# A decode kernel's K and V in pieces of 48, 32 and 48 KB over a ring lapped twice per head

## Chip, cores and metric

One core of one Trainium2 chip. The metric is the device time of one launch in microseconds (us), the median of the runs. Each run also gives the span, from the first to the last instruction that the profile counts.

## The reference, cut to what matters

One token of a transformer block: layer norm, grouped-query attention over a cache of 65,536 positions, an output projection and a small gated feed-forward part. Eight K/V heads serve 32 query heads.

```python
Hq, Hkv, Sk, Dh = 32, 8, 65536, 128
q = (layernorm(x) @ wq)                       # one token
scores = einsum("bhqd,bhkd->bhqk", q, k) * Dh ** -0.5
o = einsum("bhqk,bhkd->bhqd", softmax(scores), v)
h = x + o @ wo
h2 = h + (sigmoid(n @ w_gate) * (n @ w_up)) @ w_down      # n = layernorm(h)
```

K and V of a head are 16 MB each; with eight heads and the weights 282 MB have to be read, each byte once.

## The kernel before

The SP engine issues all loads, in one fixed order, on one queue. K and V come in blocks of 4 MB (32 KB per partition) into a ring of four slots; K of one head is interleaved with V of the head before.

```python
order = [("wq", 0)]
order += [("K", b) for b in range(NR)]                    # NR = 4 blocks per head
for b in range(NR, NB):
    order += [("K", b), ("V", b - NR)]
order += [("V", NB - 4), ("V", NB - 3), ("V", NB - 2), ("V", NB - 1), ("wg", 0), ("wu", 0), ("wd", 0)]
# ... slot i % 4; a load waits for the user of the load four places earlier:
def freed(ld):
    k, b = ld
    return {"wq": "q", "K": f"F{b}", "V": f"PV{b}"}[k]    # K: transposed by DVE; V: multiplied by PE
```

VectorE (DVE) transposes K chunk by chunk (a chunk is 4 KB per partition; 8 to a block), TensorE (PE) multiplies them with q into scores; after four blocks the maxima are taken and the exponentials made; in the next head's time PE multiplies the transposed probabilities with V, two chunks to a round, four rounds to a block:

```python
# PE, for each head i and block r of four:
#   scores of K block (i, r)                    32 matmuls of 128x512
#   if r == 3: maxima, exponentials (section X)
#   PV of V block (i - 1, r)                    4 rounds of 8 matmuls
# ... DVE, for each chunk c of a block b:
op("dve", lambda e: e.transpose(dst, src), deps, f"T{b}.{c}", to="T")
# ... after the last one:
op("dve", lambda e: e.memset(scr[:, b:b + 1], 0.0), (), f"F{b}")   # the mark that frees the slot
```

At the end, the last four V blocks take slots of V blocks two places earlier; wo goes into the space of the transposed K; then the gate, up and down weights.

Of the kernel before, what the change touches and what calls it, by code (L numbers as in the profile page):

```python
# [13 lines left out]
HKV = 8  # L14
GS = 4
NQ = 32
DH = 128
# [18 lines left out]
class Prog:  # L36
# [26 lines left out]
    def emit(self):  # L63
# [3 lines left out]
        needed = {d for ops in self.ops.values() for o in ops for d in o["deps"]} | set(self.at_end)  # L67
# [20 lines left out]
        for e, ops in self.ops.items():  # L88
            n = 0
            for o in ops:  # L90
                if o["dma"]:
                    k, v = o["dma"]
                    value[o["name"]] = (self.dma_sems[k]["sem"], v, k)
                elif o["to"]:
                    k = o["to"]
                    counts[k] = counts.get(k, 0) + 1
                    if o["name"]:
                        value[o["name"]] = (extra[k], counts[k], k)
                    o["inc"] = True
                elif o["name"] in needed or o.get("inc"):  # L100
                    n += o["times"]
                    value[o["name"] or id(o)] = (sems[e], n, e)
                    o["inc"] = True
# [110 lines left out]
def bass_sequential_preLN__gqa_block_cached__glu_gated_glu__decode_kernel(  # L214
# [10 lines left out]
    SLOT = T * DH  # L225
    CH = TC * DH
    NF = FF // 128
# [6 lines left out]
    with ExitStack() as es:  # L234
# [16 lines left out]
        ring = sb("ring", [128, NSLOT * SLOT], bf16)  # L251
# [50 lines left out]
        def slot_ap(s):  # L302
            return ring[:, s * SLOT:(s + 1) * SLOT]

# [4 lines left out]
        order = [("wq", 0)]  # L309
        order += [("K", b) for b in range(NR)]  # L310
        for b in range(NR, NB):
            order += [("K", b), ("V", b - NR)]
        order += [("V", NB - 4), ("V", NB - 3), ("V", NB - 2), ("V", NB - 1), ("wg", 0), ("wu", 0), ("wd", 0)]
        slot_of, prev = {}, {}
        for i, ld in enumerate(order):
            if ld[0] == "V" and ld[1] >= NB - NR:
                slot_of[ld] = slot_of["V", ld[1] - 2]
                prev[ld] = ("V", ld[1] - 2)
            elif ld[0][0] == "w" and i:
                slot_of[ld] = 3 if ld[0] == "wd" else 1  # L320
                prev[ld] = ("K", NB - 1 if ld[0] == "wd" else NB - 2)
            else:
                slot_of[ld] = i % NSLOT
                prev[ld] = order[i - NSLOT] if i >= NSLOT else None

        def freed(ld):
            if ld is None:
                return None
            k, b = ld
            return {"wq": "q", "K": f"F{b}", "V": f"PV{b}"}[k]  # L330

        dma("act", lambda e: e.dma_start(x_col[:, :], A_x[0].rearrange("o (p k) -> (o p) k", k=4)), "x", name="x")
        V_SPLIT = [(0, 3), (3, 4)]
        W_SPLIT = {"wg": [(0, 4)], "wu": [(0, 3), (3, 4)]}
        W_AT = {"wg": 0, "wu": 4 * FF}
        for ld in order:
            k, b = ld
            s = slot_of[ld]
            dst = slot_ap(s)
            deps = [freed(prev[ld])]  # L340
            if k == "wq":
                dma("sp", lambda e, d=dst: e.dma_start(d.rearrange("p (k n) -> p k n", k=4),
                    A_wq.rearrange("(p k) n -> p k n", p=128)), f"r{s}", deps, "wq")
            elif k in ("wg", "wu"):
                w = B_w_gate if k == "wg" else B_w_up
                dst, src = dst[:, W_AT[k]:W_AT[k] + 4 * FF], w.rearrange("(p k) n -> p (k n)", p=128)
                for i, (k0, k1) in enumerate(W_SPLIT[k]):
                    dma("sp", lambda e, d=dst, w=src, a=k0 * FF, z=k1 * FF: e.dma_start(d[:, a:z], w[:, a:z]),
                        f"{k}{i}", deps if i == 0 else (), f"{k}.{i}")
            elif k == "wd":  # L350
                src = B_w_down.rearrange("(p r) n -> p r n", p=128)
                for i, (r0, r1) in enumerate(WD_SPLIT):
                    dma("sp", lambda e, d2=dst[:, r0 * D:r1 * D].rearrange("p (r n) -> p r n", n=D), sr=src[:, r0:r1, :]:
                        e.dma_start(d2, sr), f"wd{i}", deps if i == 0 else (), f"wd{i}")
            else:
                h, r = b // NR, b % NR
                cache = A_k_cache if k == "K" else A_v_cache
                src = cache[0, h, r * BLK:(r + 1) * BLK, :].rearrange("(p t) d -> p (t d)", t=T)
                if ld == ("V", NB - 1):
                    for i, (c0, c1) in enumerate(V_SPLIT):  # L360
                        d2, s2 = (ap[:, 2 * c0 * CH:2 * c1 * CH] for ap in (dst, src))
                        dma("sp", lambda e, d2=d2, s2=s2: e.dma_start(d2, s2),
                            "v0" if i else "vl", deps if i == 0 else (), f"V{b}.{i}")
                else:
                    dma("sp", lambda e, d=dst, sr=src: e.dma_start(d, sr), f"v{s}" if k == "V" else f"k{s}" if k == "K" and b >= NR else f"r{s}",
                        deps, f"{k}{b}")
            if ld == ("V", NB - 4):
                for i, (j0, nj) in enumerate(WO):
                    src = A_wo[j0 * DH:(j0 + nj) * DH, :].rearrange("(p r) n -> p (r n)", r=nj)
                    dst = ktw[:, j0 * D:(j0 + nj) * D]  # L370
                    dma("sp", lambda e, src=src, dst=dst: e.dma_start(dst, src), f"wo{i}",
                        [f"G{HKV - 1}"] if i == 0 else (), f"wo{i}")
# [81 lines left out]
        def project_q(e):  # L454

            e.reg_mov(reg(e, 0), addr_of(xz, 8 + 7))
            e.reg_mov(reg(e, 4), addr_of(ring, slot_of[("wq", 0)] * SLOT))
# [3 lines left out]
            with e.Fori(0, HKV):  # L461
                for kt in range(4):
                    mm_at(e, ps(1, 0, 512, 0, 8), at_reg(xz, reg(e, kt), [[4 * 16, 128], [1, 8]]),
                          at_reg(ring, reg(e, 4 + kt), [[NSLOT * SLOT, 128], [1, 512]]), False, 32)
# [36 lines left out]
        def dve_block(b):  # L501
            s = slot_of[("K", b)]
            for c in range(NC):
                n = b * NC + c
                at = s * SLOT + (2 * (c % NR) + c // NR) * CH
                src = ring[:, at:at + CH].bitcast(fp32)
                dst = ktw[:, (n % NKT) * CH:(n % NKT + 1) * CH].bitcast(fp32)
                deps = [f"K{b}"] if c == 0 else []
                if b % NR or b == 0:
                    deps.append(f"S{b - 1}.{c}" if b else None)  # L510
                op("dve", lambda e, d=dst, sr=src: e.transpose(d, sr), deps, f"T{b}.{c}", to="T")  # L511
            op("dve", lambda e: e.memset(scr[:, b:b + 1], 0.0), (), f"F{b}")
# [62 lines left out]
        def pv_regs(e):  # L575
            for half in range(NC // NR):
                for tq in range(4):
                    i = 8 * half + tq
                    if i:
                        e.reg_alu(reg(e, i), R["p"], 2 * (128 * tq + half), ALU.add)  # L580
                        e.reg_alu(reg(e, i + 4), R["v"], 2 * (half * TC + 4 * tq) * 128, ALU.add)

        def pv(b):
            h, r = b // NR, b % NR
            if r == NR - 1:
                P.part["pe"] = ("VL", b)
                op("pe", lambda e: None, [f"V{b}" if b < NB - 1 else f"V{b}.1"])
            P.part["pe"] = ("B", b)
            for half in range(NC // NR):
                for tq in range(4):  # L590
                    i = half * 8 + tq
# [3 lines left out]
                        at_reg(ring, reg(e, i + 4) if i else R["v"], [[NSLOT * SLOT, 128], [1, 512]]), False, 32, 32 * tq),  # L595
                       (), f"PV{b}" if half and tq == 3 else None, times=NR)

        def head_out(h):
            op("act", lambda e: e.activation(po_sb[:, :], ps(PO, 0, 512), AF.Copy, scale=rl[:, :]),  # L599
               [f"PV{NR * h + NR - 1}", f"rl{h}"], f"po{h}", to="po")  # L600
# [68 lines left out]
        def pe_flow(e, section):  # L669
# [7 lines left out]
            i, w, p, v, m, k = (R.setdefault(n, e.alloc_register(f"r_{n}")) for n in "iwpvmk")  # L677
            w0, p0 = addr_of(ktw, W0 + NC - 1 + 127), addr_of(PT_sb, 31 * 4)
            v_even, v_odd = (addr_of(ring, slot_of[("V", b)] * SLOT) for b in (0, 1))
            e.reg_mov(i, 0)  # L680
            goto("head")
            e.reg_mov(w, w0)
            e.reg_mov(p, p0)
            goto("part")
# [13 lines left out]
            e.reg_mov(m, NR)  # L698
            e.reg_mov(k, 0)
            e.reg_mov(v, v_even)  # L700

            def odd_late():
                e.reg_mov(v, v_odd)
                e.reg_mov(m, NR - 1)
                e.reg_mov(k, 1)
                away("br_eq", i, HKV, "last_values", lambda: section("VZ"), "sums")
                section("V3")

            def odd():
                e.reg_mov(v, v_odd)  # L710
                section("V1")

            away("br_eq", w, w0, "values0", lambda: section("V0"), "sums")
            away("br_eq", w, w0 - 4, "values1", odd, "sums")
            away("br_eq", w, w0 - 12, "values3", odd_late, "sums")
# [5 lines left out]
            e.reg_alu(p, p, 2 * 512, ALU.add)  # L721
# [5 lines left out]
            def rest():  # L727
                pv_regs(e)
                e.reg_mov(m, 1)
# [7 lines left out]
            e.reg_alu(p, p, 4 - 2 * NR * 512, ALU.add)  # L737
# [7 lines left out]
            away("br_eq", w, w0 - 4, "rows_of_o", lambda: section("L"))  # L745
# [126 lines left out]
```

## Time and profile before

| | before |
|---|---|
| time, median of the runs | 658.86 us (658.33 to 659.61) |
| span of the profiled run | 657.1 us |
| data read | 282.33 MB |
| share of 16 DMA engines' span on the data queue | 99.7% |
| PE, DVE busy | 64%, 53% |
| idle DMA time between the first and the last load (packet records), sum per engine | under 0.5 us |

The last row is from the trace's record of each DMA packet (start, duration, size). One packet here is one partition's row of a transfer; 128 packets, eight to each of 16 engines, make a transfer. The record does not name the engine; a packet that starts where another ended is taken to be on the same one. I call *lead* the time from the issue of a transfer to its first packet, and *spread* the time between its first packets on the first and on the last of the 16 engines. With a full queue the lead is long because a transfer stands behind others. The lines of the profile that carry the reading are in the prediction below.

### The profile page before, as it was taken

The page shows a single profiled execution, that of the slowest core. Times are in us where ns is not written, and L with a number is a line of the kernel's source. Part 1 is how long each engine was busy: PE and PEld are TensorE (multiplying, and loading weights), DVE is VectorE, ACT ScalarE, POOL GpSimd, SP SyncE. Part 2 cuts the span into 40 slices and gives each one's busy share as a digit, 9 for nine tenths or more (in the row PEclk, how much of TensorE's full clock was granted, in tenths as well). Part 3 has the DMA queues.
Part 4 walks back from the last instruction along what each step waited for, and adds up shares of the span by engine and source line. Part 5 has one row for each costly group of instructions (what it writes and reads, how often), then busy time and mean ns, then how long its engine had stood idle before and what let it go on. Part 6 is the DMA issues. An engine that isn't in the chain of part 4 may idle for free. (4 is left out here: it accounts for less than half of the span.)

```text
span 657.1 us, 6111 instructions
## 1 busy us (share of the span) xinstructions
PE 420.5 (64%) x2315; PEld 74.1 (11%) x1547; DVE 349.7 (53%) x439; ACT 42.9 (7%) x114; POOL 3.6 (1%) x17
## 2 busy tenths in 40 slices
PE   0688488548666585576765575764866668556746
PEld 0200011011000010010100110101100001001322
DVE  2399775547537665347555374465743575542202
ACT  1100200020000200020000200002000100002001
POOL 1000000000000000000000000000000000000000
PEclk9989689677888697776966769765888869677676
DMA  9999999999999999999999999999999999999998
GB/s 383 447 433 429 439 423 431 431 447 415 447 415 447 437 425 447 415 447 419 443 441 421 447 415 447 423 439 443 419 447 415 447 427 435 445 417 427 435 430 352
DMA packets 10802, 282.34 MB, mean 430 GB/s; under 512 B 1329, under 2 KB 1330, under 8 KB 1842
## 3 DMA queue, kind: packets, MB, share of 16 engines
q1 hardware_dynamic: 10658, 282.33, 99.7%
q10 hardware_dynamic: 144, 0.00, 0.0%
HBM read 282.33 MB, written 0.00 MB: 430 GB/s over the span
## 5 line engine op out<-in xcount | busy, mean ns | idle before, releaser
L431 PE MATMUL PS<-ktw 128*128 128x512 bf16 x1024 | 299.9, 442 | 157.4 <-DVE ktw L511 153.6
L511 DVE STREAM_TRANSPOSE ktw<-ring 128x1024 f32<-128x1024 f32 x256 | 291.6, 1205 | 128.0 <-DMA ring<-in_A_k_cache_dram 128.0
L431 PE MATMUL PS<-ring,PT_sb 128*32 x1024 | 83.9, 455 | 23.6 <-issue 13.2
L431 PEld LDWEIGHTS PS<-ktw 128*128 x256 | 27.1, 106 | 408.2 <-issue 256.8
L565 DVE STREAM_TRANSPOSE PT_sb<-P_sb 128x512 bf16<-128x512 bf16 x32 | 20.2, 684 | 54.0 <-PE PS L602 52.3
L551 ACT ACTIVATE negmax<-PS 128x1 f32<-128x1 f32 x8 | 1.4, 171 | 520.6 <-PE PS L549 520.6
L431 PEld LDWEIGHTS PS<-ring,PT_sb 128*32 x1024 | 25.8, 116 | 79.8 <-issue 74.6
L516 DVE TENSOR_REDUCE M_sb<-PS 128x1 f32<-128x512 f32 x32 | 19.9, 684 | 25.5 <-PE PS L431 25.5
L555 ACT ACTIVATE P_sb<-PS,negmax 128x512 bf16<-128x512 f32 x32 | 21.6, 686 | 0.3
L572 DVE TENSOR_REDUCE lsum<-PS 128x1 f32<-128x4 f32 x8 | 1.3, 163 | 31.2 <-PE PS L570 31.2
L542 PE MATMUL PS<-identf,gm 128*1 128x128 f32 x16 | 3.4, 301 | 16.9 <-DVE gm L540 16.9
L616 DVE TENSOR_TENSOR Lw<-O,blk_of 128x896 bf16<-128x896 bf16 (+1 forms) x2 | 1.4, 683 | 20.6 <-ACT O L606 20.6
L402 PE MATMUL PS<-st,onesf 128*128 128x2 f32 x4 | 1.2, 362 | 16.1 <-DVE st L401 16.1
L431 PE MATMUL PS<-ring,xz 128*8 x32 | 9.2, 459 | 2.3 <-issue 2.3
L599 ACT ACTIVATE po_sb<-PS,rl 128x512 bf16<-128x512 f32 x8 | 5.5, 687 | 53.2 <-PE PS L431 53.2
L431 PE MATMUL PS<-ktw,O 128*1 x26 | 7.6, 464 | 0.0
L549 PE MATMUL PS<-one_f,gmrep 1*128 1x1 f32 x16 | 4.2, 330 | 5.0 <-DVE gmrep L546 5.0
L555 ACT ACTIVATION_READ_ACCUMULATOR P_sb<-PS,negmax 128x1 f32 x32 | 6.5, 202 | 0.0
L476 DVE STREAM_TRANSPOSE qt<-qh 32x512 bf16<-32x512 bf16 x1 | 0.7, 699 | 10.6 <-ACT qh L473 10.6
L602 PE MATMUL PS<-sel_bf,po_sb 128*128 128x4 bf16 x32 | 2.0, 168 | 6.4 <-ACT po_sb L599 6.4
L417 DVE CAST hT<-x_col 128x4 f32<-128x4 bf16 x1 | 0.2, 171 | 10.6 <-DMA x_col<-in_A_x_dram 10.6
L661 DVE COPY yr<-PS 1x512 f32<-1x512 f32 x1 | 0.7, 679 | 8.3 <-PE PS L659 8.3
(82 smaller groups left out, 74.0 us busy)
## 6 DMA issues: line engine op xcount, KB each, us to landing
ring<-in_A_k_cache_dram SPq DMA_DIRECT2D x32, 4096.0 KB, 28.7
ring<-in_A_v_cache_dram SPq DMA_DIRECT2D x31, 4096.0 KB, 26.4
ring<-in_A_wq_dram SPq DMA_DIRECT2D x1, 4096.0 KB, 12.3
ktw<-in_A_wo_dram SPq DMA_DIRECT2D x1, 3584.0 KB, 12.7
ring<-in_A_v_cache_dram SPq DMA_DIRECT2D x1, 3072.0 KB, 13.2
ring<-in_B_w_gate_dram SPq DMA_DIRECT2D x1, 1792.0 KB, 19.0
ring<-in_B_w_up_dram SPq DMA_DIRECT2D x1, 1344.0 KB, 21.7
ring<-in_A_v_cache_dram SPq DMA_DIRECT2D x1, 1024.0 KB, 15.2
```

What stands on the lines that cost most here:

```text
L431: return e.add_instruction(mybir.InstMatmult(name=nc.get_next_instruction_name(), engine=mybir.EngineType.PE, ins=[rhs, lhsT], outs=[e.low ...
L511: op("dve", lambda e, d=dst, sr=src: e.transpose(d, sr), deps, f"T{b}.{c}", to="T")
L516: op("dve", lambda e, u=u: e.tensor_reduce(M_sb[:, u % 4:u % 4 + 1], ps(u % NS, 0, 512), AX.X, ALU.max), [f"S{b}.{NC - NR + k}"], f"mx{u}" ...
L542: op("pe", lambda e: e.matmul(ps(MISC, 0, 128, 0, 1), lhsT=gm[:, :], rhs=identf[:, :], start=True, stop=True), [f"gm{h}"], f"gmT{h}", to="Q")
L549: op("pe", lambda e: e.matmul(ps(MISC, 128, 129), lhsT=gmrep[0:1, :], rhs=one_f[0:1, 0:1], start=True, stop=True), [f"gmrep{h}"], f"neg{h}")
L551: op("act", lambda e: e.activation(negmax[:, k:k + 1], ps(MISC, 128, 129), AF.Copy, scale=-att_scale), [f"neg{h}"], f"negmax{h}")
L555: op("act", lambda e, b=b: e.activation(P_sb[:, (b % 4) * 512:(b % 4 + 1) * 512], ps(b % NS, 0, 512), AF.Exp, bias=negmax[:, k:k + 1], sca ...
L565: op("dve", lambda e, b=b: e.transpose(PT_sb[:, (b % 4) * 512:(b % 4 + 1) * 512], P_sb[:, (b % 4) * 512:(b % 4 + 1) * 512]), [f"E{b}", f"o ...
L572: op("dve", lambda e: e.tensor_reduce(lsum[:, :], ps(MISC, 132, 136), AX.X, ALU.add), [f"l{h}"], f"ls{h}", to="D")
L599: op("act", lambda e: e.activation(po_sb[:, :], ps(PO, 0, 512), AF.Copy, scale=rl[:, :]), [f"PV{NR * h + NR - 1}", f"rl{h}"], f"po{h}", to ...
L602: op("pe", lambda e, t=t: e.matmul(ps(OX, 0, 4), lhsT=po_sb[:, t * 128:(t + 1) * 128], rhs=sel_bf[:, 8 * t:8 * t + 8:2], start=(t == 0), s ...
L616: op("dve", lambda e: e.tensor_tensor(Lw[i][:, :].rearrange("p (j c) -> p j c", j=n), bass.AP(tensor=O2, offset=j0, ap=[[NQ, 128], [1, n], ...
```

## The change

Intent: fewer, larger transfers (six per head instead of eight), in pieces that fill a 128 KB ring exactly when it is lapped twice per head. In each lap a slot is taken again as soon as its readers are through: the first piece of V waits only until two of six rounds of the last PV group have read the end of its slot.

```diff
-        order = [("wq", 0)]
-        order += [("K", b) for b in range(NR)]
...
+    PIECES = ((0, 12), (12, 20), (20, 32))                       # chunks: 48, 32, 48 KB
+    RING = 32 * CH
+    AT = {"K": (0, 24, 8), "V": (12, 0, 20), "K0": (0, 12, 20), "wq": 24, "wg": 12, "wd": 8}
...
+        for h in range(1, HKV + 1):
+            old = h - 2
+            before_k = (["F0.1"], ["G0"], [f"F{h}.1"]) if h == 1 else ([f"PV{old}.2"], [f"PV{old}.3"], [f"F{h}.1"])
+            before_v = (["F0.3"] if h == 1 else [f"PV{old}.3:2"], [f"F{h}.0"], [f"F{h}.2"])
+            if h < HKV:
+                for q in range(3):
+                    load("K", h, q, before_k[q], ("ka", "kb", "ka")[q], f"K{h}.{q}")
+                    load("V", h - 1, q, before_v[q], ("va", "vb", "va")[q], f"V{h - 1}.{q}")
+                continue
+            load("V", h - 1, 0, before_v[0], "va", f"V{h - 1}.0")
...          (wo)
+            load("V", h - 1, 1, (), "vb", f"V{h - 1}.1")
+            for i, cols in enumerate(LAST):
+                load("V", h - 1, 2, [f"PV{h - 1}.1"] if i == 0 else (), f"v{i}", f"V{h - 1}.2{'ab'[i]}", cols)
...
-            op("dve", lambda e: e.memset(scr[:, b:b + 1], 0.0), (), f"F{b}")
+                mark = {7: 0, 11: 1, 19: 2}.get(j, 3 if b == 2 and c == 7 else None)      # j: chunk in the head
+                if mark is not None:
+                    op("dve", lambda e, m=4 * h + mark: e.memset(scr[:, m:m + 1], 0.0),
+                       [f"S{b}.{c}"] if h and mark in (1, 2) else (), f"F{h}.{mark}")
...
+        PARTS = (4, 2, 4, 6)          # PV rounds after the scores of blocks 0 to 3 (were 4 each)
...
             section("B")
-            e.reg_alu(p, p, 2 * 512, ALU.add)
+            e.reg_alu(p, p, s, ALU.add)
+            e.reg_alu(s, s, step[0] ^ step[1], ALU.bitwise_xor)
```

`PV3.3:2` reads: after the second round of the fourth PV group of head 3. Scores are still made in blocks of eight chunks, so K.2 (chunks 20 to 31) brings the second half of block 2 and all of block 3.

## The prediction

> **What bounds the kernel now.** I read the page's DMA rows first, because 282 MB in 657 us is close to what 16 engines can move at all.
>
> ```profile
> span 657.1 us, 6111 instructions
> PE 420.5 (64%) x2315; PEld 74.1 (11%) x1547; DVE 349.7 (53%) x439; ACT 42.9 (7%) x114; POOL 3.6 (1%) x17
> ...
> DMA  9999999999999999999999999999999999999998
> GB/s 383 447 433 429 439 423 431 431 447 415 447 415 447 437 425 447 415 447 419 443 441 421 447 415 447 423 439 443 419 447 415 447 427 435 445 417 427 435 430 352
> ...
> q1 hardware_dynamic: 10658, 282.33, 99.7%
> ```
>
> No compute engine is above 64%; the DMA row is full in every slice and the one queue that carries the data fills 99.7% of 16 engines' span. The swing between 415 and 447 GB/s is no slack: packets of 32 KB are booked whole into 16 us slices. I also added up the trace's packet records: between the first packet at 1.0 us and the last weight packet at 654.6 us there is no time with an idle DMA engine. So nothing can be won except bytes (unchanged) or cost per packet; a lot can be lost if the queue ever runs dry. Next, who sets when a transfer is issued (the DMA queue's own waits):
>
> ```profile
> SPq L365 <- DVE scr L512: 324.2, 30, 19.4
> SPq L365 <- PE PS L431: 222.4, 29, 18.8
> ```
>
> The issuer waits 547 us in all for slots: for DVE (K transposed) and for PE (V multiplied). These waits are harmless as long as other transfers are queued. The issues' times to landing say how many are: 28.7 us for a K block, 26.4 for a V block, where one 4 MB transfer takes 9.7. That is nearly two others ahead. Pairing the issues with the packet records, the shortest leads (issue to first packet) are 4.2 us for the tenth transfer and 3.6 us for wo; most are 12 to 23. Then the timeline near the end, where the change will matter:
>
> ```profile
> 560.10 19.44 SPq L365 DMA_DIRECT2D ring<-in_A_v_cache_dram  x2
> 564.43 9.13 DVE L511 STREAM_TRANSPOSE ktw<-ring 128x1024 f32<-128x1024 f32 x8 [9.48 <-DMA ring<-in_A_k_cache_dram]
> ...
> 566.85 0.59 PE L431 MATMUL PS<-ktw 128*128 128x512 bf16 x1 [0.51 <-DVE ktw L511]
> 567.98 0.59 PE L431 MATMUL PS<-ktw 128*128 128x512 bf16 x1 [0.54 <-DVE ktw L511]
> 569.11 7.97 PE L431 MATMUL PS<-ktw 128*128 128x512 bf16 x29 [0.54 <-DVE ktw L511]
> ...
> 577.00 2.17 PE L431 MATMUL PS<-ring,PT_sb 128*32 x32
> ...
> 583.83 9.13 DVE L511 STREAM_TRANSPOSE ktw<-ring 128x1024 f32<-128x1024 f32 x8 [10.27 <-DMA ring<-in_A_k_cache_dram]
> ...
> 596.39 2.48 DVE L516 TENSOR_REDUCE M_sb<-PS 128x1 f32<-128x512 f32 x4 [3.42 <-PE PS L431]
> ...
> 602.45 2.76 PE L431 MATMUL PS<-ring,PT_sb 128*32 x24 [1.75 <-issue]
> ...
> 606.57 8.66 SPq L365 DMA_DIRECT2D ring<-in_A_v_cache_dram  x2
> ```
>
> Two transposes that each start on a K landing are 19.40 us apart, with one K and one V transfer between: 9.70 us per 32 KB per partition, 0.303 us per KB. A chunk (4 KB) is transposed in 9.13/8 = 1.14 us. The second issue of the first line, at 579.2 us (the row's end), is the first V block of head 7: it takes the slot that the products at 577.00 have freed, well before the last V block of head 6 has landed (593.2). Lastly the chain of waits at the end: after the last V piece it is some 13 us of small PE, ACT and DVE steps beside the landing of the weights, which ends at 654.6, so both meet.
>
> **What the Trainium skill says.** "DMA: Bandwidth & Descriptors", section "Where 436 GB/s comes from", puts the fabric ceiling at 435.2 GB/s for 16 ports; the page's mean of 430 agrees. Same page, "Anatomy of one DMA": a semaphore wait happens on the issuing sequencer and "the SDMA engines just consume their queues"; so a blocked issue blocks all issues behind it, as SPq's waits here do. Same page, "Why small descriptors are slow": a fixed overhead per packet. The records agree: 24,576 B take 912 ns and 32,768 B 1213 ns, so 27.2 bytes per ns and 9 ns fixed. "TensorE: Matmul & The Clock Gate", Part 1: the array falls to half clock when idle and needs sustained work to leave it. Here the windows show a granted 0.50 for 8 to 9 us after each late K landing, then 1.00.
>
> **The change part by part.**
> Removed: 16 of the 64 K and V transfers (six per head for eight). A transfer of 8 packets per engine takes 9.685 us at the steady pace, its bytes at 27.2 per ns 9.632, so 53 ns are fixed: 16 x 0.053 = 0.85 us saved, on the bounding engines, if a 48 KB row stays one packet. If it is cut in two, that becomes a loss of about 0.5.
> Moved off the path: PV rounds are regrouped 4, 2, 4, 6 (16 as before); a register operation more per round; transposes wait in two marks for PE. None of this fills the DMA.
> Added, and decisive: which work must be done before a transfer may be issued. In the ring a head's order is K.0, V.0, K.1, V.1, K.2, V.2 (48, 48, 32, 32, 48, 48 KB; V of the head before). K.0 waits for the third group of products, V.0 for two rounds of the last group, both behind the processing of K.2. From T, the start of K.2's transposes, I rebuild it with durations of before:
> 1. 16 score matmuls of K.2's first four chunks: four start with their transposes (the last at T+4.7, from 564.43 to 569.11), then 12 more with the clock rising. The 29-matmul group lasts 7.6 to 9.1 us over the heads against 6.3 at full clock (0.217 each), so 5 to 13 run at 0.427: done at T+8.5 to 10.2, mean T+9.4.
> 2. Four PV rounds, 2.2: T+11.6. Here K.0 of the next head may go.
> 3. PE's turn from PV back to scores, 0.8 (it is so after each PV block, 104.05 to 104.83 for one): T+12.4. Then 32 matmuls at 0.217 = 7.0: T+19.4. The 12 transposes end at T+13.7, so they don't bound.
> 4. The maxima start 0.6 before the last score: T+18.8. From the first maximum to the first PV matmul of the last group 596.39 to 602.45 = 6.06: T+24.9.
> 5. Two rounds, 16 of 24 matmuls that took 2.76 = 1.84: T+26.7. Issue to first packet about 1.0 (the first load): T+27.7. T is 0.34 after the last byte of K.2, so 28.1 after it.
> In the middle of the run two 48 KB pieces (V.2, next K.0) lie between K.2's end and V.0: 2 x 14.5, less 0.3 by which transfers overlap, = 28.7. It fits with 0.6 us to spare; K.0's wait (11.6 + 1.0 + 0.3 = 12.9 against 14.2) with 1.3. Only late clock rises (0.8 over the mean) give gaps of 0.2 us: 0.3 us in all.
> In the last round there is no next K.0. V.0 of head 7 follows V.2 of head 6 at once, and still waits for those two rounds: 28.1 needed, 14.2 there. The DMA engines stand idle for 13.9 us. wo and V.1 stand behind it in the same queue. Restart: the first transfer of the run took 10.6 from its first packet to the next one's, not 9.7: 0.9. Afterwards the stream is without gaps (V.2's wait for PV.1 ends some 6 us after V.0 lands, with wo and V.1, 19 us, still to move), so all is shifted to the end; the final chain changes by perhaps 0.1.
> Sum: 13.9 + 0.9 + 0.3 - 0.85 - 0.1 = 14.1; 659.4 + 14.1 = 673.5 us.
>
> **The rivals.**
> First, hidden anyway: the pieces keep the engines fed everywhere and the time falls by the 0.85 us of packets, to 658.5. For it: every lead of before is above 3.5 us, and the ring has the same 128 KB. Against: V.0's slot in the last round holds the end of K.2 and the start of V.2, which can't be free earlier than 12 transposes (13.7 us) after K.2 lands, and that alone exceeds the budget.
> Second, a wait in each head: if path 1 to 5 is 1 us longer than I have it, six heads lose some 0.4 us each besides the last, which loses 1.0: 677. For it: spare of 0.6 us, and PE's clock is the least certain term. Against: the steps are taken from spans that recur within 0.2 us in all heads except the clock's rise.
> Third, PE becomes the bound, since groups of six rounds and half-block scores make it wait in larger lumps. Against: 64% busy, and at half clock for much of it; its backlog is gone by the next K.2, where it waits some 9 us. That would need over 77 us of work per head, and there are some 52. I give it little.
> Fourth, a 48 KB row pitch makes reading faster or slower. The packet times of 24, 28 and 32 KB rows lie on one line; I expect 1.81 us for 48 KB.
>
> **Range and chances.** 2% slower begins at 672.6, 0.9 us below the estimate. The clock (plus or minus 0.7), the restart (0.5) and the fixed steps (0.6) give about 1.1; errors upward are amplified by the second rival. So 671 to 677 in 8 of 10. Chances: faster 0.01 (nothing to win there), within 2% 0.31, slower 0.68.
>
> **What would show it.** In the profile after: one slice near 600 us with DMA far under 9, the others full; idle time of 13 to 15 us between V.2 of head 6 and V.0 of head 7; SPq's V.0 issue about 27 us after the start of K.2's transposes in each head; all other leads at least 1 us; 48 KB packets of 1.81 us. It would be wrong if the dip were missing, or came in each head, or if PE's clock did not rise within the first half-block.

## The result

The changed kernel takes 698.31 us (697.58 to 699.18, 4 runs), before 658.86 us. The ratio is 1.0598 (95% interval 1.0578 to 1.0619); a ratio is the mean time of one kernel's runs over that of the other's in the same rounds, so it is not quite the quotient of the medians. It is slower, as I thought likelier, but by 39.5 us where I had worked out 14.1, and outside my range.

The rows of the page of the changed kernel that answer to those of before:

```profile
span 697.7 us, 6265 instructions
...
DMA  9999999899999999999999999999999999918997
GB/s 421 417 446 414 436 375 428 364 409 431 444 417 409 404 426 445 375 397 425 442 426 380 417 424 443 423 380 403 441 434 392 395 431 439 434 82 333 421 429 335
...
q1 hardware_dynamic: 8354, 282.33, 95.5%
```

The same bytes in fewer packets (8,354 for 10,658), and a queue at 95.5%. One slice has nearly no traffic: that is the predicted dip at the end. But ten of the other slices have 364 to 404 GB/s, where before had none under 415 between its first and last slice. The loss looks small in the share (4%) because the slow packets, of which more below, count as busy.

The waits of the DMA queue:

```profile
SPq L324 <- DVE scr L500: 304.2, 23, 15.2
SPq L324 <- PE PS L416: 293.7, 20, 35.9
```

The waits for PE grew from 222 to 294 us, and one of them is 35.9 us long. It is V.0 of head 7, as the timeline at the end shows (start, duration, engine, instruction):

```profile
594.62 36.56 SPq L324 DMA_DIRECT2D ring<-in_A_v_cache_dram  x2
602.87 13.76 DVE L497 STREAM_TRANSPOSE ktw<-ring 128x1024 f32<-128x1024 f32 x12 [8.28 <-DMA ring<-in_A_k_cache_dram]
...
612.69 1.60 PE L416 MATMUL PS<-ring,PT_sb 128*32 x24
...
622.75 2.48 DVE L505 TENSOR_REDUCE M_sb<-PS 128x1 f32<-128x512 f32 x4 [6.12 <-PE PS L416]
...
628.79 4.61 PE L416 MATMUL PS<-ring,PT_sb 128*32 x40 [1.73 <-PEq L171]
631.23 0.91 SPq L343 DMA_DIRECT2D ktw<-in_A_wo_dram  x2
```

The two issues of the first line are V.2 of head 6 at 594.6 and V.0 of head 7 at 630.9, two PV rounds after 628.79. What that does to the DMA engines is plain in a table by stretch, whose last two columns are the share of the 16 engines and GB/s:

```profile
594.00:608.00 14.00, 2.71 (x8) 0.21 (x2) 5.19 (x6) 0.00 (x0) 0.00 (x0) 0.66 1.01 435
608.00:618.00 10.00, 8.66 (x53) 1.30 (x37) 8.62 (x8) 0.00 (x0) 0.00 (x0) 0.79 0.58 251
618.00:632.00 14.00, 9.53 (x57) 1.70 (x41) 3.14 (x8) 2.95 (x9) 0.00 (x0) 0.78 0.13 39
632.00:646.00 14.00, 2.87 (x30) 0.98 (x22) 3.81 (x7) 1.35 (x3) 0.00 (x0) 0.62 0.94 400
```

The chain of waits now runs through it as well, where before it was all small steps of the compute engines:

```profile
628.79 2.05 PE PS L416 x12
630.84 0.02 issue
630.86 17.74 DMA ring<-in_A_v_cache_dram
```

That explains some 14 us, as predicted. The other 25 are in the heads. Here is head 2 in the changed kernel, from K.2's landing; it is the quickest of the seven:

```profile
198.87 13.63 DVE L497 STREAM_TRANSPOSE ktw<-ring 128x1024 f32<-128x1024 f32 x12 [9.91 <-DMA ring<-in_A_k_cache_dram]
...
203.55 4.14 PE L416 MATMUL PS<-ktw 128*128 128x512 bf16 x13 [0.54 <-DVE ktw L497]
207.62 1.60 PE L416 MATMUL PS<-ring,PT_sb 128*32 x24
209.61 0.63 PE L416 MATMUL PS<-ring,PT_sb 128*32 x8 [0.39 <-issue]
210.28 0.33 SPq L324 DMA_DIRECT2D ring<-in_A_k_cache_dram  x1
211.24 7.10 PE L416 MATMUL PS<-ktw 128*128 128x512 bf16 x32 [1.00 <-DVE ktw L497]
217.73 2.48 DVE L505 TENSOR_REDUCE M_sb<-PS 128x1 f32<-128x512 f32 x4 [5.22 <-PE PS L416]
...
223.77 6.00 PE L416 MATMUL PS<-ring,PT_sb 128*32 x48 [1.93 <-PEq L171]
225.83 0.33 SPq L324 DMA_DIRECT2D ring<-in_A_v_cache_dram  x1
```

Counted from T = 198.87, the start of the transposes, the next K.0 is issued at T+11.4 and V.0 at T+27.0. I had worked out T+11.6 and T+26.7, so in this head the path of compute was right to 0.3 us. The other heads are later. In head 4, for example, the two issues come at T+12.6 and T+28.1:

```profile
360.24 13.76 DVE L497 STREAM_TRANSPOSE ktw<-ring 128x1024 f32<-128x1024 f32 x12 [8.23 <-DMA ring<-in_A_k_cache_dram]
...
372.87 0.33 SPq L324 DMA_DIRECT2D ring<-in_A_k_cache_dram  x1
...
388.37 0.33 SPq L324 DMA_DIRECT2D ring<-in_A_v_cache_dram  x1
```

Over heads 1 to 6 the means are T+12.2 and T+27.8, so V.0 is 1.1 us later than I had it. That alone can't account for the loss in a head, as e6 and e7 will show. Each head takes more: V.0 of heads 1 and 6 are issued at 146.7 and 549.1 us, 80.5 us per head, against 77.5 (256 KB at 0.303).

The packet records show what happens at these two issues. All 16 engines were busy with V.2 when K.0 was issued at 210.28; the fastest of them got its first packet of K.0 at 211.28, just when it had finished. The first packets of that transfer took mostly 2.1 to 2.8 us each, where 1.815 is normal, and the 16 engines started on it over 1.7 us. The table pools the transfers of 24 KB rows and more (without each run's first one) of all 14 traces, by lead:

| lead | transfers | packet time over normal, us per engine and transfer | spread (median), us |
|---|---|---|---|
| under 1.3 us | 74 | 0.77 | 1.5 |
| 1.3 to 2.5 | 18 | 0.42 | 2.1 |
| 2.5 to 4 | 49 | 0.02 | 1.05 |
| over 4 | 640 | 0.006 | 1.05 |

In the kernel before the spread is 0.3 us, no transfer after the first has a lead under 2.5, and no packet is slow. In the changed kernel 14 transfers have a lead under 1.3 (K.2 of head 1, K.0 of heads 2 to 7, and every V.0 from head 1 on) and their spread is 0.7 to 3.3 us. Through the last head it stays at 3.2 to 3.5 us.

### The profile page after: what moved, and what is told of

It is laid out like the page before. It is cut to its first block, busy times and chain, and to the rows that moved or that the text cites. A ratio compares the mean times of both kernels' runs of the same rounds, so it can differ in the third digit from the quotient of the medians.

```text
span 697.7 us, 6265 instructions
## 1 busy us (share of the span) xinstructions
PE 425.4 (61%) x2315; PEld 69.9 (10%) x1547; DVE 350.4 (50%) x432; ACT 42.9 (6%) x114; POOL 3.6 (1%) x17
## 3 DMA queue, kind: packets, MB, share of 16 engines
q1 hardware_dynamic: 8354, 282.33, 95.5%
## 5 line engine op out<-in xcount | busy, mean ns | idle before, releaser
L416 PE MATMUL PS<-ktw 128*128 128x512 bf16 x1024 | 295.3, 438 | 171.8 <-DVE ktw L497 166.8
L416 PE MATMUL PS<-ring,PT_sb 128*32 x1024 | 91.0, 462 | 44.1 <-PEq L171 25.3
L416 PEld LDWEIGHTS PS<-ring,PT_sb 128*32 x1024 | 21.7, 116 | 118.4 <-issue 114.9
L500 DVE MEMSET scr<- 1x1 f32 x25 | 1.5, 59 | 45.6 <-PE PS L416 45.6
L587 ACT ACTIVATE po_sb<-PS,rl 128x512 bf16<-128x512 f32 x8 | 5.5, 687 | 77.5 <-PE PS L416 77.5
L461 DVE STREAM_TRANSPOSE qt<-qh 32x512 bf16<-32x512 bf16 x1 | 0.7, 699 | 11.3 <-ACT qh L458 11.3
## 6 DMA issues: line engine op xcount, KB each, us to landing
ring<-in_A_wq_dram SPq DMA_DIRECT2D x1, 4096.0 KB, 12.2
ring<-in_B_w_gate_dram SPq DMA_DIRECT2D x1, 1792.0 KB, 28.1
```

Source lines behind the costliest of these rows:

```text
L416: return e.add_instruction(mybir.InstMatmult(name=nc.get_next_instruction_name(), engine=mybir.EngineType.PE, ins=[rhs, lhsT], outs=[e.low ...
L500: op("dve", lambda e, m=4 * h + mark: e.memset(scr[:, m:m + 1], 0.0), [f"S{b}.{c}"] if h and mark in (1, 2) else (), f"F{h}.{mark}")
L587: op("act", lambda e: e.activation(po_sb[:, :], ps(PO, 0, 512), AF.Copy, scale=rl[:, :]), [f"PV{h}.{NR - 1}", f"rl{h}"], f"po{h}", to="po")
```

## The experiments

**Theory.** Two things cost: the idle stretch at the end, some 14 us, and in each head two issues that come when the queue is all but empty. Such an issue costs some 1.5 us even where it comes in time for its first packet (estimated from the loss: 25 us over 14 to 16 such issues). **Rival A**: rows of 48 KB are slow in themselves. **Rival B**: the regrouped PV rounds, with one register operation more each, bound PE and so the heads. In the table, lost time is the sum over the profiled run, per engine, of idle time between the first and last load and of packet time over normal; leads count transfers of 24 KB rows and more. The times of before were 658.3 to 658.9 us in all rounds.

| run | time, us | ratio to before | mean span, us | leads under 1.3 us | idle + slow, us |
|---|---|---|---|---|---|
| before | 658.9 | 1 | 657.0 | 0 | 0.4 + 1.2 |
| after | 698.3 | 1.060 | 697.0 | 14 | 28.6 + 13.5 |
| e1_tail | 687.1 | 1.045 | 683.0 | 11 | 10.2 + 13.2 |
| e2_early | 678.6 | 1.029 | 676.5 | 3 | 18.0 + 3.9 |
| e3_both | 667.6 | 1.016 | 663.5 | 2 | 3.2 + 2.5 |
| e4_six | 712.3 | 1.082 | 711.0 | 12 | 44.0 + 11.3 |
| e5_ahead | 662.2 | 1.006 | 658.2 | 0 | 0.4 + 1.1 |
| e6_four | 670.3 | 1.017 | 665.0 | 6 | 4.3 + 5.6 |
| e7_sixclean | 675.4 | 1.027 | 670.9 | 6 | 8.7 + 6.1 |
| e8_v0free | 674.3 | 1.023 | 672.5 | 7 | 7.6 + 7.9 |
| e9_late6 | 666.3 | 1.012 | 664.8 | 6 | 3.3 + 4.8 |
| e10_late5 | 664.2 | 1.009 | 662.5 | 4 | 2.2 + 3.1 |
| e11_late4 | 659.4 | 1.003 | 658.5 | 0 | 0.4 + 0.9 |
| e12_halves | 669.0 | 1.016 | 664.4 | 3 | 4.7 + 4.5 |

(The mean span of before is of its runs beside the first four experiments, 656.8 to 657.4.) One thing in the table no view explains: in e1, e3, e5, e6, e7 and e12 the time is mostly 4.4 to 5.4 us above the span, in the others mostly 1.3 to 2.4. These six have the moved V of the last head, with a few more register operations on PE. The difference lies outside what the profile counts, so for them I go by spans. Some of these kernels also scatter more from run to run: the spans of e3 lie between 661.0 and 666.9, those of e6 between 661.8 and 667.1, where before stays within 656.7 and 657.4. The packet records are of one run of each.

**e1_tail.** The last head's V goes where the next K would have gone.

```diff
+    AT = {..., "V7": (0, 12, 20), "wg": 0, ...}
-            load("V", h - 1, 0, before_v[0], "va", f"V{h - 1}.0")
+            load("V", h - 1, 0, [f"PV{old}.2"], "va", f"V{h - 1}.0")
+            # PE: in the last head V is read from chunks 0 and 12; V.2 has a semaphore of its own
```

> Edit: the last head's V goes where the next K would have gone (chunks 0, 12 and 20), so V.0 of head 7 waits for the third group of products of head 6 (as each K.0 does) and not for two rounds of its last group. Theory (transfers that are issued when the queue is all but empty cost time, twice per head, and the last head has one idle stretch of 14.5 us besides): only the long stretch goes, the two late issues of each head stay: 698.3 - 14 = 684, and the page's one slice with DMA 1 is gone. Rival A (packets of 48 KB are slow in themselves, or PE's regrouped rounds bound the run): also about 684, since the stretch is no matter of packets; it tells how much of the 39.5 us is the end alone. If the theory of the tail is wrong: 698.

687.1 us; the mean span fell from 697.0 to 683.0, by 14.0 (the four spans of e1 lie between 681.0 and 685.7). So the idle stretch is worth some 14 us as predicted, and some 26 us are elsewhere. It tells nothing between the rivals, as expected.

**e2_early.** V.1 is multiplied before K.2 arrives.

```diff
-        PARTS = (4, 2, 4, 6)
+        PARTS = (6, 4, 0, 6)
-            ... [f"PV{old}.2"] ...                        # next K.0
+            ... [f"F{h - 1}.3", f"PV{old}.1"] ...         # F.3: chunk 23 transposed
```

> Edit: rounds in groups of 6, 4, 0, 6: V.1 is multiplied before the scores of K.2, so the next K.0 waits for it no longer (it waits for four transposes of K.2 instead), and the last group comes about 3 us earlier. Theory of late issues: both late issues of a head become early (leads of 8 and about 3 us), engines stay in step, heads take 77.3 us again; left are the end (V.0 of head 7 at some 25 us after K.2, 14 are there: 11 idle, 1 restart) and a late issue or two in head 1: 671 to 674. Rival A (48 KB packets slow in themselves): the 48 KB pieces are all still there, so 690 or more. Rival B (PE's loop with its further register operation bounds the heads): rounds are the same number, so 690 or more.

678.6 us, 19.7 below the changed kernel and 5 above the range that I expected. From head 2 on the records show what the theory says: leads of 7.8 us and more for K.0 and 2.2 to 2.9 for V.0, and nearly all 48 KB packets at 1815 ns. Head 1 still had two late issues (its K.2 2.5 us after the last engine was through), which I had put at less. Rivals A and B, which asked for 690 or more, fall: the rows are still 48 KB and PE does the same rounds (in three groups now, not four).

**e3_both.** e1 and e2 together.

```diff
+    # AT["V7"] and the last head's waits as in e1
+        PARTS = (6, 4, 0, 6)
```

> Edit: e1 and e2 together. Theory: no late issue after head 1, no idle stretch at the end: 657.5 to 660, at or a little under the kernel before (16 transfers fewer at 53 ns each are 0.85 us). Rival A or B: 676 or more.

667.6 us, mean span 663.5: 8 to 10 over what I expected. Some 3 are further time outside the span (4.6 us on the mean, 1.5 in before). The profiled run, with a span of 661.1, has 4 us more than before, and its only late issues are two in head 1 (leads 0.96 and 0.96; 1.1 us of idle time of all engines besides). Why three of the six runs took 2 to 6 us longer than that one isn't known; they weren't profiled.

**e4_six.** The named part of the change undone: V.0 waits for all six rounds.

```diff
-            before_v = (["F0.3"] if h == 1 else [f"PV{old}.3:2"], ...
+            before_v = (["F0.3"] if h == 1 else [f"PV{old}.3"], ...
```

> Edit: V.0's slot is taken only after all six rounds of the last group, not after two (the named part of the change is undone). Four rounds at the half clock are about 4 us. Theory: that issue is on the path in each head, so each of seven heads and the end lose 4 us: 698.3 + 8 x 4 = 730. Rival A (slow packets, the wait itself is hidden): 698 to 702.

712.3 us: 14 more, not 32. The issue is on the path (rival A's 702 is passed), but V.0 at T+31.3 on the mean, 3.5 us later, cost 2.2 per head (82.7 between V.0 issues, 80.5 in the changed kernel), and the idle stretch of the last head grew by 3.2. With a full stop in each head, the engines stood idle together, and at the end of the V.0 transfers they were 1.1 to 1.3 us apart rather than 1.3 to 3.2, so perhaps part of what the spread had cost was got back. That explanation is from the records alone; I did not test it by itself.

**e5_ahead.** e3 with the two late waits of head 1 made early and one semaphore fewer.

```diff
-            ... [f"F{h}.1"] ...  [f"F{h}.2"] ...
+            ... [f"F{h}.1", f"PV{h - 1}.0"] ...  [f"F{h}.2", f"PV{h - 1}.1"] ...
-                       [f"S{b}.{c}"] if h and mark in (1, 2) else (), f"F{h}.{mark}")
+                       (), f"F{h}.{mark}")
```

> Edit: e3 without a third V semaphore, and with the two waits that were still late in head 1 made early (K.2 and V.2 wait for the V products themselves, not for a mark of VectorE behind half a block of scores). e3's profile has a span of 661.1 with two late issues, both in head 1, and 1.4 to 3.8 us more outside the span than before has. Theory: no issue has a lead under 2 us, engines stay in step, span 656 to 657.5, so 657.5 to 659 us if the time outside the span was the semaphore's, else 660 to 662. Rival (engines come out of step by themselves with 48 KB pieces): span 660 or more though all leads are long.

The profiled run has a span of 656.9 us (the five 656.9 to 660.2), no lead under 2.7 us, and the page is full again:

```profile
span 656.9 us, 6300 instructions
...
DMA  9999999999999999999999999999999999999998
...
DMA packets 8499, 282.35 MB, mean 430 GB/s; under 512 B 1073, under 2 KB 1074, under 8 KB 1586
```

So with long leads the whole loss of the change is gone in the profiled run, while its ring and its 48 KB rows remain; the mean span, 658.2, is 1.3 us above that of before. The time is 662.2 us, still 0.6% above before (interval 0.5 to 0.7), mostly because of the 1.9 to 4.9 us outside the span; the semaphore was not their cause. The 0.85 us that fewer packets should save do not show: the last load ends at 654.39 us, at 654.56 in before, with a spread of 1.05 in place of 0.3 and one slow transfer of 0.35 in head 1. This was the version that I hoped would beat both kernels; it doesn't beat before.

**e6_four and e7_sixclean.** e5, with V.0 waiting for four and for six rounds instead of two.

```diff
-            ... [f"PV{old}.3:2"] ...
+            ... [f"PV{old}.3:4"] ...      # e6;  [f"PV{old}.3"] in e7
```

> Edit: e5, but V.0 of each head waits for four rounds of the last group and not for two: 1.9 us later, the lead falls from about 3 to about 1.1 us in six heads, which is what an issue takes to its first packet. Theory of the prediction (a lead of 1.0 suffices): as e5 within 1 us. Theory of late issues (an issue into an all but empty queue costs by itself): 0.5 to 1.5 us per head more, 3 to 9 us over e5.

> Edit: e5, but V.0 waits for all six rounds: 3.8 us later, so 0.8 us after the moment at which the fastest engine runs dry, 1.8 with the way from issue to packet. Idle alone: 6 heads x 1.8 = 11 over e5. With a restart of about 0.9 on top: 6 x 2.7 = 16 over e5.

This is the dose to the disputed step. e6: the leads of six V.0 fall from about 3.35 to about 0.97. The mean span rises by 6.8 us and the median time by 8.1. The profiled span rises by 9.8, of which 1.4 lie behind the last load (it ends at 662.80, in e5 at 654.39). That is 1.1 to 1.4 us per issue, the upper part of the expected 0.5 to 1.5, where "a lead of 1.0 suffices" asked for nothing. V.0 is issued at T+26.2 here, earlier than I had planned it, and still costs this much. At the first of them the fastest engine waited about 0.1 us, so lateness alone is not it. e7: 13.0 us (mean 12.7), 2.1 per issue, with V.0 at T+28.1; the transfer comes 1.9 us later than in e6 and costs only about 0.8 more. That lies between the two expectations, 11 and 16.

**e8_v0free.** The changed kernel with 16 KB more ring, so that V.0 no longer waits for PV rounds.

```diff
-    RING = 32 * CH
+    RING = 36 * CH
-    AT = {..., "V": (12, 0, 20), ...}
+    AT = {..., "V": (12, 0, 24), ...}
-            ... [f"PV{old}.3:2"] ...
+            ... [f"F{h - 1}.3"] ...        # F.3: all of K.2 transposed
```

> Edit: the changed kernel with 16 KB more ring: V.2 lies behind the rest, so V.0 waits only for the transposes of K.2 (13 us earlier), and the next K.0 still for the products of V.1 behind half a block of scores. It takes away one of the two late waits of a head and nearly all of the idle stretch at the end. Theory: with the V.0 wait gone engines are disturbed once per head; 14.5 + 1 to 2 of 39 us are the end's, of the remaining 24 half go: 668 to 675. If K.0's wait is harmless when alone: 659 to 662. If it was the costly one: 680.

674.3 us, in the range. It tells that K.0's wait alone is costly: V.0 has leads of 14 us and more from head 1 to 6, K.0 of heads 2 to 7 under 1.0, and nearly 16 us over before remain with seven such issues, V.0 of the last head among them (two more in head 1 with leads of 1.6 and 2.2).

**e9_late6, e10_late5, e11_late4.** The kernel before, with nothing changed but one wait: the first K block of heads 2 to 7 is held until seven, six or five of eight transposes ahead of it are done.

```diff
+                if b % NR == NR - 1 and c == 6:                   # 5 in e10, 4 in e11
+                    op("dve", lambda e: e.memset(scr[:, 40 + b // NR:41 + b // NR], 0.0), (), f"M{b // NR}")
...
+            if k == "K" and b % NR == 0 and b >= 2 * NR:
+                deps.append(f"M{b // NR - 1}")
```

> Edit: the kernel before, but the first K block of heads 2 to 7 is issued only after seven of the eight transposes of the block ahead of it (8.0 us after their start), which is 1.0 us before the queue runs dry; its lead was 19 us. Six issues; the data, the order and everything else are as before. If a lead of 1.0 suffices (my prediction): 658 to 660. If an issue into an all but empty queue costs 1.6 us by itself, as e6 against e5 says: 6 x 1.6 = 10, 667 to 670; it would then have nothing to do with the new ring or with 48 KB pieces.

> As e9 with six transposes: the lead is 2.1 us. If the cost sets in below some 3 us: between, 2 to 6 us over the kernel before. If only below 1: as before.

> As e9 with five transposes: the lead is 3.3 us. In e5 leads of 3.3 to 3.4 cost nothing (all packets 1815 ns), so 658 to 660 by both theories; if it is slower, the mark on VectorE costs and not the late issue.

The timeline of before has this issue at 186.36 us, 19 us ahead of its first packet. In e9 it waits for the mark after the seventh transpose:

```profile
197.54 9.17 DVE L513 STREAM_TRANSPOSE ktw<-ring 128x1024 f32<-128x1024 f32 x8 [10.25 <-DMA ring<-in_A_k_cache_dram]
205.49 0.06 DVE L515 MEMSET scr<- 1x1 f32 x1
205.60 0.33 SPq L367 DMA_DIRECT2D ring<-in_A_k_cache_dram  x1
```

666.3 us: six issues with leads of 0.95 cost 7.9 us, 1.3 each, in a kernel with the old ring, 32 KB rows and the old PE loop. Their packets took 1283 to 1302 ns on the mean where 1213 is normal. e11: five transposes, a lead of 2.74 in the profile (I had worked out 3.3), and 659.4 us, 0.3% over before (interval 0.1 to 0.5): the mark and this lead together cost about 1 us over six issues, a small part of the 7.9. e10 was meant to have a lead of 2.1; its profile shows 0.95 to 1.7; its engines were up to 2.6 us out of step, so the fastest one ran dry earlier and the block ahead landed later. It cost 5.9 us. So it gives no point at 2.1, but fits the feedback described below.

**e12_halves.** e6 with each 48 KB piece as two transfers of 24 KB rows behind the same wait.

```diff
+            cuts = (a, a + 6, z) if z - a == 12 else (a, z)
+            for n, (c, d) in enumerate(zip(cuts, cuts[1:])):
+                dma("sp", ..., sem, deps if n == 0 else (), ...)
```

> Edit: e6, with each 48 KB piece as two transfers of 24 KB per partition behind the same wait. It asks whether the cost of a late issue is one packet's length (the engine's next packet has to be there while the one before is still moving). If so, packets of 0.9 in place of 1.8 us make a lead of 1.1 cost about half: 4 to 5 us over e5 in place of 9.8, less 0.8 lost on more transfers. If the cost is a fixed 1.6 us per late issue: as e6, span 666 to 668.

669.0 us, mean span 664.4 (e6: 670.3 and 665.0); profiled span 666.2. It looks like e6, so shorter packets don't halve the cost. It is not quite clean: in the profile, which is 1.8 us above the mean span, the first late issues had leads of 2.0 to 2.1 and cost 0.1 to 0.7 us, and the later ones fell to about 1.0 (one has 1.8) as the engines came out of step.

## Why the prediction was wrong

**What bounds the kernel, and that nothing could be won**: right. No version here is faster than before.

**The end**: right in sum. 13.9 idle and 0.9 for the restart were predicted; the first packet of V.0 came 14.5 us after the last of V.2, and e1 is worth 14.0. Part of that is luck: the path was 1.2 us longer there than planned, and V.2 landed 0.6 later.

**Path 1 to 5**: too short, by 0.6 us for K.0 and 1.1 for V.0 on the mean. In heads 1 to 6 K.0 was issued at T+11.4 to T+12.6 and V.0 at T+27.0 to T+28.1, for T+11.6 and T+26.7; in the last head V.0 went at T+28.0. The clock's rise, the least certain term, was nearly as I had it (the 16 scores ended at T+9.6 on the mean, for 9.4). The four rounds took 2.6 in place of 2.2, the turn to the scores 1.0 in place of 0.8, the last two rounds 2.1 in place of 1.84. So V.0's spare of 0.6 us was gone.

**48 KB packets**: right, 1815 ns for the 1.81 I gave, uncut. The 0.85 us of saving did not show even in e5.

**The step that failed** is the one after the path: "It fits with 0.6 us to spare; K.0's wait (11.6 + 1.0 + 0.3 = 12.9 against 14.2) with 1.3. Only late clock rises (0.8 over the mean) give gaps of 0.2 us: 0.3 us in all." The term of 0.3 measured about 26 us: 697.0 - 657.0 = 40.0 in mean span, less 14.0 for the end. It was wrong in three ways, the first of them the largest in the runs.

First, I took a lead of 1.0 us, the way from issue to first packet, as enough. It is enough to be in time for the first engine, but such a transfer costs 1.1 to 1.4 us all the same (e6 against e5, e9 against before), of which on the mean about 0.77 is slow packets and the rest idle time of engines that got theirs later. Leads of 2.5 to 4 us were free of it in nearly all cases (0.02 us of slow packets on the mean of 49 transfers, at most 0.35 in one). By my own sum e6's V.0, at T+26.2, fits (26.2 + 1.0 + 0.3 = 27.5 against 28.7), and it cost 6.8 us in six heads. I had the restart as 0.9 us in the sum, but only once, for the end.

Second, I counted the budget from the landing of K.2 with the engines in step (0.3 us). Late issues set them apart by 1 to 3.5 us, and in these runs nothing brought them together again while they were all busy: the spread stays constant over whole heads in e3 (1.25 us), e5 (1.05) and e11 (0.78). A landing is counted when the slowest engine is through, while the fastest runs on. In head 2, shown above, the fastest took its first packet of V.2 at 196.72 and so needed K.0 at 211.2 (14.5 later), while the slowest ended K.2 at 198.49: 12.7 us were left, for 14.2 in my budget, and K.0's wait took 12.8. So a late issue makes the next one later; that chain is read from the records and fits e10, but no run tests it alone.

Third, path 1 to 5 was 1.1 us longer for V.0 than I had it. By my own sum that is a gap of some 0.5 us in each of six heads, about 3 of the 26 us. e7 agrees that this is the smaller part: its V.0 comes as late, at T+28.1, and costs 12.7 us in six heads.

The wait in each head was my second rival, at 677 us. Its premise, a path 1 us longer than I had it, came true on the mean; but it priced the wait at some 0.4 us in each head and 1.0 in the last, and the loss was 1.6 to 1.9 us for each of 14 to 16 late issues. Rivals A and B are refuted by e2 and e5, and e9 shows the cost in the old kernel. My first rival (hidden anyway) and the third (PE bound) are refuted by the dip and by e5.

**What stays open**: why the first packets of such a transfer are slow (late descriptors, or reads that no earlier packet overlaps); e12 speaks against the packet's length alone. How the 26 us divide between slow packets, engines out of step and the longer path in the changed kernel itself: the runs show only that a late issue costs by itself (e6, e9). And the 3 us outside the span in the kernels with the moved V.

## What to carry to other kernels

In a kernel that lives off the DMA queue, look at the lead of each issue over what is still queued, not at whether the engines look busy: leads near 1.0 us cost 1.1 to 1.4 us per issue here, leads of 1.3 to 2.5 still slowed the packets by 0.42 us on the mean, and the engines that such an issue set apart ate into the margin of the next one. Check a planned path against every head, not against the one that agrees: here head 2 alone fitted the plan. When a ring is planned, list for each load what its slot's last reader waits for, and look at the last round on its own: a neighbour that hid a wait all along may be missing there. Move the reader ahead of the late arrival (as e2 did) before you cut waits finer.

## What the Trainium skill lacked or had wrong

- "DMA: Bandwidth & Descriptors", "Latency and other measured facts", has about 600 ns to the first byte for a DMA issued from SP. Here the first load of each run began 1.02 to 1.06 us after the start of its issue, and V.0 of the last head, after the idle stretch, 0.95 (the packet's start, so not quite the same thing).
- The same page says to issue early ("Rules for kernel authors") but not how early. Here leads of 2.5 us and more cost next to nothing (0.02 us of slow packets on the mean), leads near 1.0 cost 1.1 to 1.4 us each.
- No page that I read says that the 16 engines come out of step after such an issue and stay so: spread 0.3 us in the kernel before, up to 3.5 in the changed one.
- The page's bandwidth tables stop at transfer sizes and say nothing of large rows: a 48 KB row moved in one packet of 1815 ns, a 32 KB row in 1213.
